# TensorE's first work in a two-branch kernel: four activation groups of the first tokens in four banks, loads in the order tokens, expert rows, tokens, weights

## The chip, the cores and the metric

The kernel runs on one core of one Trainium2 chip. The metric is the device time of one execution in microseconds (us), as the median of several runs. TensorE is written PE, VectorE DVE, ScalarE ACT, GpSimd POOL and SyncE SP, as the profile does.

## The reference

The output mixes two branches over 2048 tokens of width 576, with a gate per token. Branch A is a long convolution per channel whose kernel comes from a state space with 128 states. Branch B routes each token to experts by product keys, and is where most of TensorE's time goes:

```
def _B_ref(x, w_q, k1, k2, u, v):
    q = jnp.einsum("nd,dhc->nhc", xf, w_q)             # 32 heads, two halves of 128
    s1 = jnp.einsum("nhd,ed->nhe", q1, k1)             # 64 keys for each half
    s2 = jnp.einsum("nhd,ed->nhe", q2, k2)
    ... top 2 of s1, top 2 of s2, top 2 of their 4 sums: top_s, top_e
    g = _softmax(top_s, axis=-1)
    act = _gelu(jnp.einsum("nd,nhkd->nhk", xf, u[top_e]))
    out = jnp.einsum("nhk,nhk,nhkd->nd", g, act, v[top_e])

g = sigmoid((x * gate_w).sum(-1))
return g * a + (1 - g) * b
```

There are 64 x 64 = 4096 experts, with rows u and v of width 576.

## The kernel before, in words

**Branch B is computed densely.** The keys are folded into the query weights, so that scores are tokens times a folded matrix (`s` groups: 8 column blocks c times 16 token tiles t, one PSUM bank of 128x512 each). Activations of all experts are tokens times u (`a` groups: 8 expert blocks c times 4 token blocks tb of 512 times 4 quarters j, one bank each). Every operand is split into a high and a low float16 part, so a group is a `triple` (line 850) of 14 matmuls of 512 columns: four 128-row slices of the width 576 times three products (high-high, high-low, low-high), and two more for the last 64 rows. A score group goes to DVE (8 MAX8 and 8 FIND_INDEX8, `scores_top`, line 866). An activation group is scaled by ACT or DVE into a tile `go` and stored to DRAM (`act_post`, line 1247). Later the one-hot products `S` place gates and activations, and the products `o` with v give the output. Branch A runs beside this: a kernel generator on POOL, ACT and DVE (`kP`, `kb`), a first stage (`u`, `k`) and products in frequency (`pr`, `pi`, `pv`).

**One Python planner writes the order.** `body` keeps a clock for TensorE and a `free` time for each other engine; tasks are generators in a heap, and each is resumed when the planner's cost table says that its operands are ready. The main loop (line 1563) puts the next score or activation group on TensorE by rules on DVE's lag and on how many groups of each kind are done. Each engine's program is then a fixed list, run in order, and the waits are semaphores. So a change of the first tasks moves every later instruction a little. All loads and stores stand in SP's one list (line 204).

**The start, before.** SP issues the keys `kt`, the first token block (`xs`, 128x4x512, and its last 64 rows twice in `xr`), two halves of the first query weights `wq`, then the first expert block (`us`, `ur`), then the constants `cst` and the second token block. `x_build(0)` squares the tokens, sums squares on TensorE with a matrix of ones (`x`, five matmuls), derives a power-of-two scale (`root_scale`, line 345: four small DVE operations), and makes the high parts `xb` (TENSOR_SCALAR) and low parts (SCALAR_TENSOR_TENSOR). `w_half` folds the keys into each half of the weights (`w_fold`: 36 small float32 matmuls `wb` on TensorE, each of which is two rows of the trace), finds its scale (`wn`) and makes `whl`. `u_build(0)` does for the experts what `x_build` does for tokens and makes `uhl`, with the last 64 rows in `wrem`. TensorE's first large groups are the scores `s0`, which need `xb` and all of `whl`.

PSUM has eight banks, handed out as tags: four `sc` (for `s` and `a` groups) and four `kb` at this stage. A tag is taken at `bank()` and given back when the reader is done.

Of the kernel before, what the change touches and what calls it, by code (L numbers as in the profile page):

```python
# [116 lines left out]
class Engine:  # L117


    def __init__(self, eng, ready, clock, key, cost):  # L120
        self.eng, self.ready, self.clock, self.key, self.cost = eng, ready, clock, key, cost
        self.free = 0.0

    def __getattr__(self, op):
        f = getattr(self.eng, op)

        def call(*a, **k):
            out = k.get("out", a[0] if a else None)
            aps = [x for x in (*a, *k.values()) if x is not out and hasattr(x, "tensor")]
            start = max(self.free, self.clock[0], *(self.ready.get(self.key(x), 0.0) for x in aps))  # L130
            self.free = start + self.cost(op, out, a, k)
            self.ready[self.key(out)] = max(self.free + 0.28, self.ready.get(self.key(out), 0.0))
# [5 lines left out]
def body(ctx: ExitStack, tc: tile.TileContext, xT, au, par, logdt, dskip, gatew, wq, kT, uT, vv,  # L138
# [283 lines left out]

    def x_load(tb):
# [3 lines left out]
        dma(a, xT[0:512, c].rearrange("(k p) n -> p k n", p=128))  # L427
        dma(r[0:64], xT[512:576, c])
        dma(r[64:128], xT[512:576, c])
        return a, r  # L430
# [15 lines left out]
    def x_build(tb):  # L446
        while tb and tb - 1 not in scaled:
            yield 0.3
        if tb:
            yield from need("slot", 2)  # L450
            xl[tb] = x_load(tb)
        a, r = xl.pop(tb)
        while tb and 0 not in uhl:
            yield 0.3
        b = slot([9, 512], F16, f"xb{tb}")
        sq = b[:, 0:5].bitcast(BF16)
        yield from ready(a, r)
        if tb:
            S.activation(sq[:, 0:4, :], a, AF.Square)
        else:  # L460
            S.activation(sq[:, 0:2, :], a[:, 0:2], AF.Square)
            V.tensor_mul(sq[:, 2:4, :], a[:, 2:4], a[:, 2:4])
        S.activation(sq[:, 4, :], r, AF.Square)
        yield from ready(b)
        yield from need("kb")
        p = bank("kb", f"x{tb}")
        for k in range(5):
            mm(p, onesb, sq[:, k, :], k == 0, k == 4)
        yield from ready(p)
        V.tensor_reduce(out=nx[:, tb:tb + 1], in_=p, axis=AX, op=OP.max)  # L470
        free("kb", nx)
        s, i = root_scale(nx[:, tb:tb + 1], 1.02)
        V.tensor_copy(i_x[:, tb:tb + 1], i)
        yield from ready(s)
        for o, i in [(b[:, k], a[:, k, :]) for k in range(4)] + [(b[:, 8], r)]:
            if tb == 0 or S.free > V.free + 2.0:
                V.tensor_scalar(o, i, s, None, op0=OP.mult)
            else:
                S.activation(o, i, AF.Copy, scale=s)
        scaled.append(tb)  # L480
        for k in range(4):
            yield from ready(b)
# [1201 lines left out]
```

## Time and profile before

| what | value |
|---|---|
| median of 3 runs | 1469.38 us (1467.86 to 1471.87) |
| profiled execution: its own time | 1466.58 us |
| profiled execution: span of instructions | 1464.7 us |
| PE busy | 1431.2 us, 98% of the span |
| DVE busy | 1248.5 us, 85% |
| ACT busy | 790.6 us, 54% |
| POOL busy | 532.0 us, 36% |

The profiled execution lies 1.88 us over its span, and 2.80 us under the median. The page gives busy time by engine and by slices of the span; a view by windows gives the same for stretches that one chooses, with the clock that TensorE was granted (PEclk) and what the DMA engines moved. A row of the timeline holds the start, the duration, the engine, the operation, its tiles and its count, and in brackets the idle time before it and what ended it. Matmul durations overlap, since matmuls are pipelined: the pace is the distance from start to start.

### The profile page before, as it was taken

What the parts mean: (1) busy time and instruction counts of PE and PEld (TensorE: products, weight loads), DVE (VectorE), ACT (ScalarE), POOL (GpSimd) and SP (SyncE); (2) the same over time, 40 slices, a digit from 0 to 9 for tenths busy, and PEclk for the clock granted to TensorE, in tenths of its full rate; (3) what the DMA queues carried; (4) which work ended last, traced back from release to release, by engine and by line L of the source; (5) the groups of instructions that cost most, each with busy time, mean ns of one, the idle gap of its engine ahead of it and who ended that gap; (6) DMA issues with size and microseconds to landing.
All of it is one profiled execution on the core that took longest, in us unless ns stands there. A gap on an engine that the chain in (4) does not pass through costs nothing.

```text
span 1464.7 us, 36789 instructions
## 1 busy us (share of the span) xinstructions
PE 1431.2 (98%) x14025; PEld 858.4 (59%) x14028; DVE 1248.5 (85%) x4589; ACT 790.6 (54%) x1315; POOL 532.0 (36%) x511
## 2 busy tenths in 40 slices
PE   5999999999999999999999999998999999999999
PEld 2445454554544544555555444455787787788787
DVE  6989989989999699959899898579998998898860
ACT  5647767698697787434656544576424224223310
POOL 0443545556745645201246799622100110110100
PEclk8999999999999999999999999999999999999999
DMA  9235433372434534384768666677533432442400
GB/s 319 81 93 162 128 94 118 111 213 89 147 104 133 160 107 135 109 263 138 254 211 290 232 200 206 221 239 221 157 111 116 133 125 85 138 147 68 156 10 17
DMA packets 139185, 221.21 MB, mean 151 GB/s; under 512 B 11648, under 2 KB 82688, under 8 KB 132608
## 3 DMA queue, kind: packets, MB, share of 16 engines
q1 hardware_dynamic: 138912, 218.78, 46.5%
q8 instruction: 110, 1.80, 0.5%
q14 instruction: 67, 0.55, 0.1%
q10 hardware_dynamic: 96, 0.07, 0.0%
HBM read 147.51 MB, written 71.30 MB: 149 GB/s over the span
## 4 chain that ended last, share of the span: by engine, by line
PE 84%; DVE 10%; DMA 3%; ACT 1%; issue 1%; SPq 1%; POOL 1%; DVEq 0%; ACTq 0%; POOLq 0%
PE o L213 24%; PE a L213 23%; PE s L213 22%; PE S L213 4%; PE wb L213 2%; PE kb L213 2%; DVE i L133 2%; PE pr L213 2%; DVE m L133 1%; PE u L213 1%; PE y L213 1%; PE kP L213 1%; DVE e L133 1%; PE pv L213 1%; DVE uh L133 1%
## 5 line engine op out<-in xcount | busy, mean ns | idle before, releaser
L213 PE MATMUL o<-vhl,wh 128*128 128x288 f16 x3072 | 387.0, 286 | 0.0
L213 PE MATMUL s<-whl,xb 128*128 128x512 f16 x1536 | 369.5, 382 | 5.0 <-DVE whl L133 4.2
L213 PE MATMUL a<-xb,uhl 128*128 128x512 f16 x1536 | 361.1, 379 | 0.4 <-DVE ko L133 0.4
L213 PEld LDWEIGHTS <-wh 128*128 128x128 f16 x3072 | 296.0, 98 | 76.3 <-issue 3.7
L213 PEld LDWEIGHTS <-xb 128*128 128x128 f16 x1792 | 171.8, 98 | 213.1 <-issue 27.1
L213 PEld LDWEIGHTS <-uhl 128*128 128x128 f16 x1536 | 148.2, 98 | 175.7 <-issue 2.8
L133 DVE FIND_INDEX8 i<-m,s 128x8 uint32<-128x64 f32 x1024 | 206.5, 222 | 0.0
L133 ACT ACTIVATE wh<-gl,s_wg 128x1024 f16<-128x1024 f32 x64 | 68.9, 1137 | 200.3 <-DVE gl L133 200.3
L133 DVE MAX8 m<-s 128x8 f32<-128x64 f32 x1024 | 146.4, 215 | 28.1 <-PE s L213 27.8
L133 POOL TENSOR_TENSOR CS<-CS,ex 128x512 f32<-128x512 f32 x72 | 100.2, 1423 | 139.0 <-DVE ex L133 120.0
L133 POOL TENSOR_TENSOR ya<-ya,db 128x576 f32<-128x576 f32 x16 | 32.0, 2012 | 305.2 <-DMA ya<-in_au_dram 143.6
L133 ACT ACTIVATE go<-a,i_a 128x512 f32<-128x512 f32 x95 | 64.2, 686 | 82.5 <-PE a L213 54.7
L133 POOL TENSOR_TENSOR e<-aN,rt 128x512 f32<-128x512 f32 x72 | 87.5, 1234 | 50.9 <-PE kb L213 47.6
L133 DVE SCALAR_TENSOR_TENSOR wh<-gl,s_wg,wh 128x1024 f16<-128x1024 f32 x64 | 92.4, 1474 | 11.3 <-ACT wh L133 11.3
L133 DVE TENSOR_TENSOR gl<-S,gl 128x256 f32<-128x256 f32 x256 | 90.0, 415 | 7.3 <-PE S L213 7.3
L133 DVE TENSOR_TENSOR Bg<-Be,vals 128x1024 f16<-128x1024 f16 x128 | 90.6, 749 | 2.2
L133 ACT ACTIVATE gl<-gl 128x1024 f32<-128x1024 f32 x64 | 63.5, 1045 | 34.8 <-DMA gl<-g_d 34.8
L133 DVE TENSOR_TENSOR A<-iota_a,vals 128x2048 f16<-128x2048 f16 x64 | 80.5, 1258 | 0.0
L213 PE MATMUL S<-Bg,A 128*128 128x64 f16 x2048 | 73.0, 193 | 5.1 <-DVE Bg L133 4.2
L213 PEld LDWEIGHTS <-A 128*128 128x128 f16 x2048 | 70.6, 97 | 11.2 <-DVE Bg L133 4.1
L213 PE MATMUL s<-wrem,xb 128*128 128x512 f16 x256 | 76.2, 379 | 0.0
L213 PE MATMUL a<-xb,wrem 128*128 128x512 f16 x256 | 76.2, 379 | 0.0
(203 smaller groups left out, 2205.7 us busy)
## 6 DMA issues: line engine op xcount, KB each, us to landing
g_d<-go SPq DMA_DIRECT2D x128, 256.0 KB, 2.7
gl<-g_d SPq DMA_DIRECT2D x32, 1024.0 KB, 5.4
wq<-in_wq_dram SPq DMA_DIRECT2D x16, 1152.0 KB, 6.3
us<-in_au_dram SPq DMA_DIRECT2D x64, 144.0 KB, 3.0
su_d<-us SPq DMA_DIRECT2D x32, 288.0 KB, 2.6
sk_d<-k1o SPq DMA_DIRECT2D x32, 288.0 KB, 2.8
vn<-in_vv_dram SPq DMA_DIRECT2D x32, 288.0 KB, 3.7
ui<-su_d SPq DMA_DIRECT2D x16, 576.0 KB, 4.0
```

Source lines behind the costliest of these rows:

```text
L133: return f(*a, **k)
L213: T.matmul(o, l, r, start=start, stop=stop)
```

## The change

The loads of the first tokens and of the first expert block are issued ahead of everything else, each as two halves of 128x2x512 behind its remainder; then the keys, the second token block, the weights, the constants. Before the main loop stands a new piece of program that issues the four groups a(0,0,0..3) together, each in its own `sc` bank: for each slice of tokens, four matmuls, one for each bank; first all nine products with the high part of the experts, then the five with the low part. The first scale of tokens and of experts is taken from the sum of all squares that ACT accumulates (`scale_first`), so that it does not wait for the five `x` matmuls. The folds of the weights wait until the second token block is scaled, and lie between these groups. Tokens blocks 1 to 3 get their low parts as each slice is ready, and the second half of a weight block is loaded ahead of the next expert block. The planner's model of an engine that reads what it wrote itself is 0.16 us shorter.

The diff, cut to its core:

```
 class Engine:
+    def at(self, n):
+        t = self.ready.get(n, 0.0)
+        return t - 0.16 if self.own.get(n) == t else t
...
+    def halves_load(a, src, c):
+        columns.add(a.tensor.name)
+        for m in (0, 2):
+            dma(a[:, m:m + 2], src[128 * m:128 * m + 256, c].rearrange("(k p) n -> p k n", p=128))
...
+    def x_first():
+        a, r = xl.pop(0)
+        b = slot([9, 512], F16, "xb0")
+        first_u[1] = b
+        ahead.append(slot([9, 512], F16, "xb1"))
+        sq = ahead[0][:, 0:5].bitcast(BF16)
+        s, i = yield from scale_first(a, r, sq)
+        spawn(x_norm(0, sq))
+        V.tensor_copy(i_x[:, 0:1], i)
+        for k in range(5):
+            while k == 2 and not marks["s"]:
+                yield 0.1
+            o, lo, src = (b[:, k], b[:, 4 + k], a[:, k, :]) if k < 4 else (b[:, 8], b[64:128, 8], r)
+            p = slice(0, 128) if k < 4 else slice(64, 128)
+            V.tensor_scalar(o, src, s, None, op0=OP.mult)
+            V.scalar_tensor_tensor(lo, src[p], s[p], o[p], op0=OP.mult, op1=OP.subtract)
+            marks["x"].append(V.free + 0.28)
...
+    def scale_first(a, r, sq, keep=None):
+        acc = [newcol() for _ in range(3)]
+        yield from ready(r)
+        S.activation(sq[:, 4], r, AF.Square, accum_out=sc[:, acc[0]])
+        for n, m in enumerate((0, 2)):
+            yield from ready(a[:, m:m + 2])
+            S.activation(sq[:, m:m + 2], a[:, m:m + 2], AF.Square, accum_out=sc[:, acc[n + 1]])
+        yield from ready(sq)
+        yield from need("kb")
+        p = bank("kb", "sq")
+        for n in range(3):
+            mm(p[:, 0:1], onesb, short(acc[n].start, 1), n == 0, n == 2, 0.05)
+        yield from ready(p)
+        out = root_scale(p[:, 0:1], 1.02)
...
+    def fold_first(h, w, pbs):
+        while len(folded) < h or 1 not in scaled:
+            yield 0.2
+        out = []
+        yield from need("kb", 3 + h)
+        yield from w_fold(0, h, w, out, ("kb",) * 3)
+        pbs.extend(out)
+        folded.append(h)
...
     def w_half(c, h, w):
...
+        if c == 0:
+            spawn(fold_first(h, w, pbs))
+        while 1 not in scaled:
+            yield 0.2
...
     def u_build(c):
...
+        if c:
+            yield from need("raw")
+            while second:
+                yield 0.3
+                yield from need("raw")
+            take("raw", "raw")
...
+        if c == 0:
+            for k in range(4):
+                S.activation(hl[:, 0, k, :], a[:, k, :], AF.Copy, scale=s)
+                marks["h"].append(S.free + 0.28)
+            S.activation(rem[:, 0, :], r, AF.Copy, scale=s)
...
+            rdy[key(hl)] = marks["h"][k]
+            V.scalar_tensor_tensor(hl[:, 1, k, :], a[:, k, :], s, hl[:, 0, k, :], op0=OP.mult, op1=OP.subtract)
+            marks["u"].append(V.free + 0.28)
...
-    dma(kt, kT)
-    xl = {0: x_load(0)}
+    xl = {0: x_load(0)}
+    take("raw", "raw")
+    xl["u"] = u_load(0)
+    dma(kt, kT)
+    xl[1] = x_load(1)
     w_load(0, 0)
     w_load(0, 1)
+    dma(cst, cst_d[:, :KT])
...
+    until(lambda: marks["x"] and marks["h"], 0.1)
+    first = [bank("sc", f"a0_0_{j}") for j in range(4)]
...
+    for w, n in ((0, 9), (1, 5)):
+        for xk in [x for k in range(4) for x in (k, 4 + k)[:2 - w]] + [8]:
+            k = 4 if xk == 8 else xk % 4
+            landed("x", k)
+            landed("hu"[w], k)
+            for j in range(4):
+                cs = slice(128 * j, 128 * j + 128)
+                mm(first[j], wrems[0][:, w, cs] if k == 4 else first_u[0][:, w, k, cs], first_u[1][:, xk, :],
+                   w == 0 and xk == 0, w == 1 and k == 4)
+            pump()
+    del acts[0:4]
+    for j in range(4):
+        spawn(act_post(0, 0, j, first[j]))
     while groups or acts:
```

SP's list at its start, before (a number in a name ahead of the underscore is the block, behind it a serial number):

```order
L204 DMA kt_113<-in_kT_dram 128x128
L204 DMA xs0_119<-in_xT_dram 128x4x512
L204 DMA xr0_120<-in_xT_dram 64x512 x2
L204 DMA wq0_0_124<-in_wq_dram 128x2304
L204 DMA wq0_1_126<-in_wq_dram 128x2304
L204 DMA us0_142<-in_uT_dram 128x4x512
L204 DMA ur0_143<-in_uT_dram 64x512 x2
L204 DMA cst_70<-in_cst_dram 128x576
L204 DMA xs1_210<-in_xT_dram 128x4x512
```

and of the change:

```order
L211 DMA xr0_119<-in_xT_dram 64x512 x2
L211 DMA xs0_118<-in_xT_dram 128x2x512 x2
L211 DMA ur0_125<-in_uT_dram 64x512 x2
L211 DMA us0_124<-in_uT_dram 128x2x512 x2
L211 DMA kt_113<-in_kT_dram 128x128
L211 DMA xs1_131<-in_xT_dram 128x4x512
L211 DMA xr1_132<-in_xT_dram 64x512 x2
L211 DMA wq0_0_136<-in_wq_dram 128x2304
L211 DMA wq0_1_138<-in_wq_dram 128x2304
```

The experts' block moved ahead of the weights, and the second token block too; both first blocks come in halves.

ACT's list from its first squares on, before (`wj` are squares of the weights, `uhl0` squares and then the high parts of the experts):

```order
L133 ACTIVATE xb0_136<-xs0_119 128x1024
L133 ACTIVATE xb0_136<-xr0_120 128x512
L133 ACTIVATE wj0_0_163,sc_75<-wq0_0_124 128x1152 x2
L133 ACTIVATE wj0_1_223,sc_75<-wq0_1_126 128x1152 x2
L133 ACTIVATE whl0_135<-wb0_0_2_167,sci_76 128x2x256
L133 ACTIVATE wrem2_116<-wb0_0_4_168,sci_76 64x128 x4
L133 ACTIVATE uhl0_282,sc_75<-us0_142 128x2048
L133 ACTIVATE uhl0_282,sc_75<-ur0_143 128x512
```

and of the change:

```order
L140 ACTIVATE xb1_149,sc_75<-xr0_119 128x512
L140 ACTIVATE xb1_149,sc_75<-xs0_118 128x1024 x2
L140 ACTIVATE uhl0_150,sc_75<-ur0_125 128x512
L140 ACTIVATE uhl0_150,sc_75<-us0_124 128x1024 x2
L140 ACTIVATE uhl0_150<-us0_124,sci_76 128x512 x4
L140 ACTIVATE wrem0_114<-ur0_125,sci_76 128x512
L140 ACTIVATE vals_80<-kt_113 128x128
L140 ACTIVATE xb1_149<-xs1_131 128x2048
L140 ACTIVATE xb1_149<-xr1_132 128x512
L140 ACTIVATE xb1_149<-xs1_131,sci_76 128x512 x4
L140 ACTIVATE wj0_0_271,sc_75<-wq0_0_136 128x1152 x2
L140 ACTIVATE wj0_1_313,sc_75<-wq0_1_138 128x1152 x2
```

The squares of the weights moved behind the second token block, and the experts' high parts ahead of both.

PE's list where its large groups begin, before:

```order
L213 MATMUL wn0_1_272<-sc_75,onesb_71 128x1
L213 LDWEIGHTS onesb_71
L213 MATMUL sq_297<-sc_75,onesb_71 128x2
L213 LDWEIGHTS xb0_136
L213 MATMUL s0_0_314<-whl0_135,xb0_136 128x512
```

and of the change:

```order
L220 MATMUL sq_177<-sc_75,onesb_71 128x1
L220 LDWEIGHTS uhl0_150
L220 MATMUL a0_0_0_198<-xb0_148,uhl0_150 128x512
L220 LDWEIGHTS uhl0_150
L220 MATMUL a0_0_1_199<-xb0_148,uhl0_150 128x512
L220 LDWEIGHTS uhl0_150
L220 MATMUL a0_0_2_200<-xb0_148,uhl0_150 128x512
```

The scores `s0` behind both folds are replaced by activation groups ahead of them, one matmul for each bank in turn. Behind the 56 matmuls of these four groups the list of the change has the four groups of the second token block and then the first score group; the 72 fold matmuls `wb` lie in between, 36 behind 40 of the 56, 36 within the second token block. Counted over PE's whole list, both kernels have 1792 matmuls of `s`, 1792 of `a`, 576 of `wb`, 20 of `x`, 2048 of `S` and 3072 of `o`; the change has 13 of `sq` instead of 8. When the last score matmul is issued, 308 matmuls of `a` are left before, and 476 of the change; when the first `S` is issued, 134 and 159.

161 lines of the change are left out of this document (104 added, 57 removed).

## The prediction

> **What bounds the kernel now.** I read the page first (busy time, slices, the chain that ended last), then windows over the start, then its timeline, then the waits of TensorE behind the start.
>
> ```profile
> PE 1431.2 (98%) x14025; PEld 858.4 (59%) x14028; DVE 1248.5 (85%) x4589; ACT 790.6 (54%) x1315; POOL 532.0 (36%) x511
> ...
> PE   5999999999999999999999999998999999999999
> ...
> PE 84%; DVE 10%; DMA 3%; ACT 1%; issue 1%; SPq 1%; POOL 1%; DVEq 0%; ACTq 0%; POOLq 0%
> ```
>
> TensorE is busy for 98% of the span, carries 84% of the chain, and only its first slice is half empty. The windows say how the start differs from the rest:
>
> ```profile
> 0.00:30.67 30.67, 13.54 (x168) 8.19 (x168) 19.71 (x55) 21.02 (x35) 0.20 (x4) 0.83 0.93 331
> 30.67:100.00 69.33, 69.17 (x322) 31.48 (x324) 66.85 (x350) 35.39 (x55) 28.42 (x19) 1.00 0.31 94
> ```
>
> The first figures behind the length are PE's busy time, then PEld, DVE, ACT, POOL, the granted clock, DMA share and GB/s. In the first 30.67 us TensorE works 13.54 us, and DMA is 93% busy; after that it works without a gap. So the place to gain is the start, and what is gained there reaches the end only if TensorE stays the engine that sets the pace. The timeline of the start:
>
> ```profile
> 6.84 1.06 ACT L133 ACTIVATE xb<-xs 128x1024 bf16<-128x1024 f32 x1 [3.75 <-DMA xs<-in_xT_dram]
> 7.95 2.29 PE L213 MATMUL x<-xb,onesb 128*128 128x512 bf16 x5 [4.54 <-ACT xb L133]
> 10.90 3.38 PE L213 MATMUL wb<-kt,wq 128*64 128x64 f32 x72 [0.66 <-DMA wq<-in_wq_dram]
> 11.01 0.15 DVE L133 TENSOR_SCALAR sc<-nx 128x1 f32<-128x1 f32 x1
> 11.71 1.67 DVE L133 TENSOR_SCALAR xb<-xs,sci 128x512 f16<-128x512 f32 x4
> 12.08 1.17 ACT L133 ACTIVATE wj<-wq 128x1152 bf16<-128x1152 f32 x1
> 13.15 0.19 ACT L133 ACTIVATION_READ_ACCUMULATOR wj<-wq 128x1 f32 x1
> 14.35 2.32 PE L213 MATMUL wb<-kt,wq 128*64 128x64 f32 x72
> 15.23 0.74 DVE L133 SCALAR_TENSOR_TENSOR xb<-xs,sci,xb 128x512 f16<-128x512 f32 x1
> 20.84 0.16 PE L213 MATMUL sq<-sc,onesb 128*128 128x2 bf16 x1 [4.04 <-ACT uhl L133]
> 23.47 2.56 ACT L133 ACTIVATE uhl<-us,sci 128x512 f16<-128x512 f32 x4
> 26.34 4.50 PE L213 MATMUL s<-whl,xb 128*128 128x512 f16 x11 [4.20 <-DVE whl L133]
> 30.67 0.59 PE L213 MATMUL s<-wrem,xb 128*128 128x512 f16 x2
> 31.30 1.15 DVE L133 MAX8 m<-s 128x8 f32<-128x64 f32 x8 [2.38 <-PE s L213]
> ```
>
> TensorE's large groups begin at 26.34 (one matmul earlier, at 21.55), because the scores wait for the last low part of the folded weights, `whl`. The eleven matmuls take 4.3 us from start to start, twice their later pace, and these windows show why (0.50 and 1.00 are the granted clock):
>
> ```profile
> 20.10:30.34 10.24, 4.75 (x12) 1.63 (x12) 8.29 (x18) 8.78 (x16) 0.00 (x0) 0.50 0.98 352
> 30.34:40.00 9.66, 9.61 (x45) 4.36 (x45) 7.63 (x62) 3.68 (x6) 0.00 (x0) 1.00 0.53 166
> ```
>
> So the dense stretch at full pace begins at 30.67, with 12 score matmuls, both folds and the norm of the first tokens already done.
>
> **The change, part by part: when the new groups can start.** The loads come first. Bytes by time are read from windows of two microseconds (last figure GB/s), and one landing from the DMA issues:
>
> ```profile
> 0.00:2.00 2.00, 0.00 (x0) 0.10 (x1) 1.00 (x6) 1.26 (x1) 0.20 (x4) 1.00 0.08 22
> 2.00:4.00 2.00, 0.27 (x1) 0.10 (x1) 0.45 (x2) 0.54 (x3) 0.00 (x0) 1.00 0.73 165
> 4.00:6.00 2.00, 0.00 (x0) 0.00 (x0) 0.00 (x0) 0.00 (x0) 0.00 (x0) 1.00 1.04 401
> 6.00:8.00 2.00, 0.05 (x1) 0.04 (x1) 1.16 (x1) 1.16 (x2) 0.00 (x0) 1.00 1.08 345
> 8.00:10.00 2.00, 2.00 (x5) 0.50 (x4) 0.07 (x1) 0.42 (x1) 0.00 (x0) 1.00 1.01 415
> ```
>
> ```profile
> xs<-in_xT_dram SPq DMA_DIRECT2D x1, 1024.0 KB, 5.6
> ```
>
> Two microseconds of each give 0.04, 0.37, 1.18, 1.87 and 2.70 MB by 2, 4, 6, 8 and 10 us. The keys and `xs` are 1.11 MB, moved by 5.8 us; `xs` was issued at 1.19 and landed at 6.8, so a landing is told 1.0 us after its last byte. In the new order tokens are 1.31 MB, landed at 7.4, and tokens with experts 2.62 MB, moved by 9.8 and landed at **10.8 us**. From there on, by the rows above: ACT squares the last half, 1.06, and reads its sum (that row ends 0.10 behind the square): 12.0. Three `sq` matmuls and their way to DVE, about 0.3 as in the row of `sq`: 12.3. `root_scale`, 0.70 from 11.01 to 11.71: 13.0. ACT makes the first high slice, 2.56/4 = 0.64: **TensorE starts at 13.65**. The tokens are no later: from 7.4, ACT 1.2, `sq` 0.3, scale 0.7 give 9.6, and two pairs of high and low slices (1.67/4 + 0.74 each) end at 11.9, before the experts' scale is wanted on DVE. The other pairs (three, 3.5 us) and the experts' low parts (five of 0.74) end near 20, well ahead of the matmuls that read them. Feeding TensorE then costs nothing: the cover is some 24 us of matmuls.
>
> The clock costs something. Before, it rose 4.0 us after the dense start at 26.34, which lost 2.0 us. The first work at 7.95 to 13.3 lost about as much (the first fold took 3.38, the second 2.32). I take 2.3.
>
> By the Trainium skill, TensorE: Matmul & The Clock Gate, section on the HAM clock gate, activity is judged in free-running windows of 3.413 us, and one busy window is needed. The 10.24 us at half clock above are three such windows, so the trace agrees. By that page the half-clock stretch lasts 3.4 to 6.8 us, an estimate of 1.7 to 3.4 us lost instead of 2.3, depending on where the windows fall.
>
> **What is done later than before.** To reach the state of 30.67, TensorE still owes the 12 score matmuls, both folds (2.3 each, 4.6) and the small `wn` and `kn` (0.4). The pace comes from the chain:
>
> ```profile
> 54.60 3.02 PE s L213 x14
> ```
>
> That is 0.216 each, so 12 are 2.6. And there is a new wait: all four groups end with the same last slice, so behind them `a_1_0` needs a bank that ACT has to empty. ACT's list is late there: it squares the second tokens, waits for their scale (TensorE reaches `x` after 24 matmuls, 13.65 + 2.3 + 5.2 = 21.2; then 1.2, 0.7 and 0.7 to 23.8), scales them for 2.6 us and squares the weights for 5.4: 31.8. TensorE ends the four groups at 13.65 + 2.3 + 56 x 0.216 + 1.1 + 2.3 + 0.2 = 31.7. Then `go` takes
>
> ```profile
> L133 ACT ACTIVATE go<-a,i_a 128x512 f32<-128x512 f32 x95 | 64.2, 686 | 82.5 <-PE a L213 54.7
> ```
>
> 0.69 us. Behind the stopped matmul stands all of TensorE's list. I take 1.5 us for this and for the second fold's banks, with bounds of 0 and 3 (four of these evictions in a row). Four banks in turn, 128x512 matmuls each, is a form that no row shows; a row of 14 in one bank has 0.216, so I take no gain and no cost.
>
> **Sum.** 13.65 + 2.3 + 2.6 + 4.6 + 0.4 + 1.5 = 25.05, against 30.67: **5.6 us less** at the start. The profiled execution took 1466.58, its span and 1.88 around it; 1466.58 - 5.6 = 1461.0. It lies 2.8 under the median of the runs, so for a median I say 1463.7.
>
> **What follows.** The planner writes the whole list anew, so every later wait is drawn again. These are TensorE's waits from 31 us on:
>
> ```profile
> PE S L213 <- DVE Bg L133: 4.2, 6, 2.3
> PE pi L213 <- DVE m L133: 1.7, 1, 1.7
> PE k L213 <- ACT k1o L133: 1.4, 1, 1.4
> PE y L213 <- DMA tf<-in_tf_dram: 1.0, 1, 1.0
> PE kb L213 <- issue: 1.0, 1, 1.0
> PE u L213 <- DVE uh L133: 0.7, 2, 0.5
> PE S L213 <- DVE ya L133: 0.7, 1, 0.7
> PE k L213 <- DVE i L133: 0.6, 1, 0.6
> ```
>
> With three smaller ones they are 12.4 us. They can fall away or come twice, so their change lies between -12.4 and +12.4; I take zero, since the numbers of matmuls are the same.
>
> **Rivals.** First, **more than the start**. Near 1000 us DVE is the bound:
>
> ```profile
> 1002.00:1060.00 58.00, 52.34 (x612) 40.04 (x610) 57.69 (x86) 27.24 (x32) 12.90 (x8) 1.00 0.60 188
> ```
>
> It works 57.69 of 58 us, and TensorE waits there 4.2 + 0.7 for `Bg` and `ya`. The change keeps 476 `a` matmuls for the time behind the scores instead of 308, which is 36 us more cover. If that removes these waits, the median is 1458.8. Against it: at the first `S` only 25 more are left, 5.4 us.
>
> Second, **the gain is eaten by new waits**: half as much again as the 12.4 us leaves 1463.7 + 6.2 = 1469.9, no change. For it: the list is in order and one late operand stops all; against it: 12.4 us in 1430 shows that the planner's costs are near the chip's.
>
> Third, **DVE becomes the bound, and it is slower**. The first MAX8 moves from 31.30 to about 52: 112 `a` and 14 `s` matmuls, ten `x`, folds and losses behind 13.65. DVE was idle for 31.3 - 19.7 = 11.6 us before its first score. Of the change it works some 32 by then (an estimate: the 67 rows of its list ahead of the first MAX8, at the durations above), and is idle for 20. If scores set the pace up to the products, the difference of some 9 us comes on top of the old time: 1469.4 + 9 = 1478. It decides once no activation group is left to fill. Against it: the spare 476 matmuls at the end of the scores.
>
> Fourth, **the early start fails**. If the experts land with the weights as late as before, TensorE starts some 3 us later: 1466.6. Or the four banks keep the clock low: 56 matmuls at half pace cost 12.1 more, less the 2.3 counted, 1473.5. The Trainium skill, TensorE: Matmul & The Clock Gate, section on psum-queue depth-cycling, reports such a clock for bursts that change banks; no run here shows it for these groups.
>
> **How the numbers follow.** The forecast, a gain of 3.5 to 8 us at the start that is kept (1461.4 to 1465.9), has 0.52. More: 0.16. Eaten: 0.20. DVE the bound: 0.08. Early start fails: 0.04. A measurement of this kernel can tell about 0.3%, 4.4 us. Faster by more than that are 0.16 and most of the forecast, 0.44, together 0.60; slower are 0.08 and 0.02; 0.30 lie between. The range takes 8 us to each side, past more cover and the eaten gain, and leaves out the worst of the bounds: 1455.5 to 1471.5.
>
> **What would show it.** First `a` matmul at 13 to 14.5 us; the granted clock full by 17.5 to 19; a wait of about 1 us for `go` near 32; first MAX8 near 52; PE at 99% of 60 to 1000 us. Wrong: more than 3 us of idle time in 13 to 50, TensorE waiting for MAX8 or FIND_INDEX8 before 1000, or waits behind 60 us that add up to 18 or more.

## The result, and the profile after

The changed kernel takes **1488.50 us** (median of 6 runs, 1484.56 to 1491.61); the kernel before, on the same chip, 1468.81 (6 runs, 1466.06 to 1471.87). The ratio is **1.013, with a 95% interval of 1.0109 to 1.015**: slower by 1.3%, where a gain of 5.6 us was forecast. The profiled execution took 1485.77 us with a span of 1484.0, which is 19.3 us more than the span before.

The page shows little of it at first sight: TensorE's share fell by one point, the first slice of PE is fuller, and only the chain of what ended last says that more of the time runs over DVE (17% against 10%) and POOL.

```profile
PE 1437.2 (97%) x14033; PEld 861.0 (58%) x14033; DVE 1255.9 (85%) x4609; ACT 777.5 (52%) x1295; POOL 533.5 (36%) x511
...
PE   6999999999999999999999999999999999999999
...
PE 73%; DVE 17%; POOL 4%; DMA 2%; issue 2%; ACT 1%; SPq 0%; DVEq 0%; POOLq 0%; ACTq 0%
```

**The start did what it was to do.** TensorE's timeline, with DVE's first MAX8 as its last row:

```profile
14.38 4.11 PE L220 MATMUL a<-xb,uhl 128*128 128x512 f16 x12 [1.44 <-ACT uhl L140]
18.39 2.75 PE L220 MATMUL a<-xb,uhl 128*128 128x512 f16 x12
...
25.60 2.32 PE L220 MATMUL wb<-kt,wq 128*64 128x64 f32 x72
27.85 2.76 PE L220 MATMUL a<-xb,uhl 128*128 128x512 f16 x12
...
32.52 0.81 PE L220 MATMUL a<-xb,uhl 128*128 128x512 f16 x3 [0.96 <-ACT go L140]
...
53.20 1.14 DVE L140 MAX8 m<-s 128x8 f32<-128x64 f32 x8
```

How far it gained is counted best by matmuls: windows of the first 60 us for the tiles `a` and `s` alone, PE's busy time with the number of matmuls in brackets. Before:

```profile
0.00:60.00 60.00, 14.98 (x68) 0.91 0.62 213
...
0.00:60.00 60.00, 17.93 (x70) 0.91 0.62 213
```

And after:

```profile
0.00:60.00 60.00, 29.39 (x124) 1.00 0.69 230
...
0.00:60.00 60.00, 9.23 (x42) 1.00 0.69 230
```

That is 166 matmuls of these groups against 138. Both kernels have done both folds, and the changed one has also done two `x` more, 17 against 15 (the trace before shows 13, but two of its three fives stand there as four in the time of five): 30 times 0.216 us are **6.5 us ahead at 60 us**. (The expectations of the experiments speak of 8 to 9 us. They were worked out with a typical duration for each kind of matmul, and that of the single `kn` held a wait; the count is right, and all their amounts lost from the start on shift by the same 2 us.)

**The loss comes behind it, in pieces.** TensorE's idle time from 60 us on is read from the windows, length minus the first figure. Before:

```profile
60.00:130.00 70.00, 69.48 (x395) 33.13 (x395) 65.47 (x353) 33.36 (x57) 32.27 (x25) 1.00 0.39 117
130.00:300.00 170.00, 170.00 (x1656) 86.41 (x1655) 153.80 (x552) 125.17 (x185) 85.32 (x69) 1.00 0.41 125
300.00:740.00 440.00, 435.68 (x4044) 224.33 (x4042) 381.49 (x1734) 304.34 (x513) 189.83 (x191) 1.00 0.49 155
740.00:960.00 220.00, 218.33 (x2054) 106.19 (x2053) 186.44 (x1119) 117.25 (x309) 164.12 (x188) 0.99 0.67 228
960.00:1090.00 130.00, 124.34 (x1381) 87.76 (x1380) 121.99 (x187) 68.69 (x89) 24.69 (x16) 1.00 0.57 181
```

After:

```profile
60.00:130.00 70.00, 64.41 (x298) 29.44 (x297) 68.73 (x384) 29.79 (x53) 29.70 (x23) 0.95 0.36 107
130.00:300.00 170.00, 166.13 (x1582) 84.61 (x1581) 159.47 (x579) 132.15 (x194) 81.86 (x66) 1.00 0.43 130
300.00:740.00 440.00, 433.57 (x4203) 223.88 (x4202) 394.31 (x1943) 288.19 (x485) 193.89 (x193) 1.00 0.43 138
740.00:960.00 220.00, 212.01 (x2000) 104.12 (x2000) 174.30 (x922) 118.18 (x319) 165.47 (x193) 1.00 0.72 239
960.00:1090.00 130.00, 123.22 (x1195) 80.09 (x1194) 113.14 (x170) 63.26 (x79) 25.38 (x14) 0.96 0.58 182
```

| us of the span | idle before | idle after | clock after, and what it cost |
|---|---|---|---|
| 60 to 130 | 0.5 | 5.6 | 0.95; two stretches of 3.4 us at half clock: 3.4 |
| 130 to 300 | 0.0 | 3.9 | 1.00 |
| 300 to 740 | 4.3 | 6.4 | 1.00 |
| 740 to 960 | 1.7 (and one stretch of 3.4 us at half clock: 1.7) | 8.0 | 1.00 |
| 960 to 1090 | 5.7 | 6.8 | 0.96; one stretch of 3.4 us and one of 6.8: 5.1 |

Behind 1090 us both work without a gap but for the last 4 us. The table's rows add up to 18.5 us of new idle time to 1090 us and 6.8 us of clock (half the length of each stretch at half clock), 25.3 of the 6.5 + 19.3 = 25.8 us that were lost. The clock is a follower: four waits of 2.1 to 3.5 us each have a stretch at half clock behind them, which costs 1.7 us, and 3.4 us after the last. In windows cut at the places where the granted clock changes:

```profile
85.40:88.80 3.40, 3.40 (x10) 1.20 (x9) 3.40 (x30) 0.00 (x0) 1.14 (x1) 0.50 0.00 0
...
1044.60:1051.40 6.80, 5.91 (x49) 4.32 (x50) 6.77 (x14) 0.00 (x0) 0.00 (x0) 0.50 0.01 2
```

The first follows the wait of 3.5 us at 80.8, the second one of 3.3 us for `Bg`. The waits of TensorE behind 60 us (total, times, longest), of 14 kinds that add up to 30.8 us:

```profile
PE S L220 <- DVE Bg L140: 6.8, 6, 3.3
PE u L220 <- DVE uh L140: 5.0, 4, 2.1
PE sq L220 <- ACT uhl L140: 3.8, 2, 3.5
PE s L220 <- DVE i L140: 2.6, 2, 2.1
```

How a wait that names ACT is DVE's: ACT's rows around 80 us, and then TensorE's.

```profile
79.90 0.26 ACT L140 ACTIVATE vals<-m 128x64 f32<-128x64 f32 x1 [2.74 <-DVE m L140]
81.49 0.26 ACT L140 ACTIVATE idx<-i 128x64 f16<-128x64 uint32 x1 [1.33 <-DVE i L140]
81.65 1.89 ACT L140 ACTIVATE uhl<-us 128x2048 bf16<-128x2048 f32 x1
83.45 0.19 ACT L140 ACTIVATION_READ_ACCUMULATOR uhl<-us 128x1 f32 x1
83.54 0.61 ACT L140 ACTIVATE uhl<-ur 128x512 bf16<-128x512 f32 x1
```

```profile
84.30 0.16 PE L220 MATMUL sq<-sc,onesb 128*128 128x2 bf16 x1 [3.51 <-ACT uhl L140]
```

ACT's list holds the copies of the first four score groups' results, for which it stands 2.74 us (MAX8) and 1.33 us (FIND_INDEX8), and the squares of the second expert block stand behind those copies. TensorE's `sq` waits for the squares, and behind `sq` stands everything else.

### The profile page after: what moved, and what is told of

Read it like the earlier page. It is cut to its first block, busy times and chain, and to the rows that moved or that the text cites. A ratio compares the mean times of both kernels' runs of the same rounds, so it can differ in the third digit from the quotient of the medians.

```text
span 1484.0 us, 36824 instructions
## 1 busy us (share of the span) xinstructions
PE 1437.2 (97%) x14033; PEld 861.0 (58%) x14033; DVE 1255.9 (85%) x4609; ACT 777.5 (52%) x1295; POOL 533.5 (36%) x511
## 4 chain that ended last, share of the span: by engine, by line
PE 73%; DVE 17%; POOL 4%; DMA 2%; issue 2%; ACT 1%; SPq 0%; DVEq 0%; POOLq 0%; ACTq 0%
PE o L220 23%; PE a L220 18%; PE s L220 18%; PE S L220 4%; DVE i L140 3%; PE wb L220 2%; POOL vf L140 2%; DVE m L140 2%; PE kb L220 2%; DVE e L140 1%; DVE uh L140 1%; DVE Y L140 1%; PE y L220 1%; DMA g_d<-go 1%; DVE CS L140 1%
## 5 line engine op out<-in xcount | busy, mean ns | idle before, releaser
L140 POOL TENSOR_TENSOR CS<-CS,ex 128x512 f32<-128x512 f32 x72 | 96.5, 1372 | 143.9 <-DVE ex L140 114.5
L140 ACT ACTIVATE go<-a,i_a 128x512 f32<-128x512 f32 x86 | 58.1, 683 | 85.3 <-PE a L220 57.5
L140 DVE TENSOR_TENSOR Bg<-Be,vals 128x1024 f16<-128x1024 f16 x128 | 86.1, 714 | 2.2
L220 PEld LDWEIGHTS <-A 128*128 128x128 f16 x2048 | 72.1, 98 | 12.6 <-DVE Bg L140 6.2
```

The lines of the kernel that those rows point to most:

```text
L140: return f(*a, **k)
L220: T.matmul(o, l, r, start=start, stop=stop)
```

## Experiments

The theories. **D**: scores start 20 us later on DVE, which then runs in debt, and TensorE waits for what stands in DVE's and ACT's lists behind score work. **L**: each newly planned list draws its own waits, and the list before is a tight one. **G**: the new gate (`while len(scaled) < 4`) holds up the second expert block. **P**: the planner's 0.16 us is too optimistic. **S**, formed later: the products S lack activation matmuls to lie between. The table holds all runs; each was compared with the kernel before on its own chip (1467.12 to 1467.92 us there). Idle time is TensorE's in the profiled execution, from windows of 60 to 960 and 960 to 1090 us, the clock that of the second.

| kernel | us | ratio, 95% interval | idle 60-960 | idle 960-1090, clock |
|---|---|---|---|---|
| before (its profile above) | 1468.81 | | 6.5 | 5.7, 1.00 |
| changed | 1488.50 | 1.013 (1.0109-1.015) | 23.9 | 6.8, 0.96 |
| a_no_gate | 1503.61 | 1.0237 (1.0216-1.0258) | 32.2 | 10.7, 0.96 |
| a_no_second | 1483.95 | 1.0108 (1.0089-1.0126) | 20.9 | 3.7, 0.99 |
| a_wire | 1485.29 | 1.013 (1.010-1.016) | 22.3 | 3.0, 1.00 |
| b_wire | 1466.86 | 0.9991 (0.9981-1.0001) | 6.6 | 4.5, 1.00 |
| a_no_index | 1479.16 | 1.0086 (1.0058-1.0115) | 18.4 | 8.7, 0.97 |
| d_b_no_index | 1466.03 | 0.9992 (0.998-1.0003) | 5.7 | 4.1, 0.99 |
| a_no_at | 1489.05 | 1.0147 (1.012-1.0174) | 9.1 | 22.3, 0.92 |
| b_at | 1498.53 | 1.0221 (1.0187-1.0256) | 29.4 | 3.8, 0.99 |
| a_weights_first | 1480.55 | 1.0085 (1.0057-1.0112) | 20.6 | 5.2, 0.97 |
| c_keep48 | 1492.85 | 1.0175 (1.0158-1.0192) | 21.4 | 16.1, 0.93 |
| c_start_only | 1477.85 | 1.007 (1.0054-1.0087) | 13.0 | 8.7, 0.97 |
| c_start_keep40 | 1485.26 | 1.0122 (1.0105-1.0138) | 25.6 | 1.7, 1.00 |
| c_b_keep40 | 1480.70 | 1.0097 (1.008-1.0114) | 20.2 | 2.2, 1.00 |
| d_b_half | 1462.08 | 0.9962 (0.9951-0.9973) | 6.9 | 4.1, 0.99 |
| d_a_half | 1471.91 | 1.0029 (1.0008-1.0049) | 10.8 | 8.0, 0.97 |
| d_start_half | 1468.78 | 1.0021 (1.0009-1.0033) | 6.2 | 7.3, 1.00 |
| e_b_no_gw | 1461.22 | 0.9949 (0.9932-0.9967) | 3.6 | 4.1, 0.99 |
| e_a_no_gw | 1463.55 | 0.9975 (0.9963-0.9987) | 5.7 | 8.5, 0.97 |

### The gates: a_no_gate and a_no_second

The changed kernel without one of its new gates each. The first:

```
-        while len(scaled) < 4:
-            yield 0.3
```

The second, in `u_build`:

```
-            while second:
-                yield 0.3
-                yield from need("raw")
```

> The changed kernel without the wait that lets the second expert block be built only when all four token blocks are scaled; its load then stands before the third token block. Theory G (the late second expert block leaves only scores behind 67 us): the waits of 3.5 and 2.1 us at 80 and 116 us and the half clock behind them go, some 8 us, so about 1480. Theory D (the first 16 score groups start 20 us later, and DVE must do them in less time before expert block 1 begins, whatever is loaded): the loss in 70 to 120 us stays at 5 to 8 us, 1485 to 1489. Theory L (each newly planned list draws its own waits): anywhere within 10 us of 1488, with waits at other places.

> The changed kernel without the rule that an expert block waits for the second half of a weight block. Up to 300 us its list is the same, so the first 8 us are lost as before. If the rule is to blame for the 8 us lost in 740 to 850 us (296 score matmuls left at the products, where 495 were left before the change), then with 523 left it is about 1480. Theory L: within 10 us of 1488, with no tie to the count of scores.

Theory G fell: without the gate the kernel is 15 us slower still, which no theory had foreseen (D's 1485 to 1489 and L's 10 us are missed as well). Its waits name DVE, as in the changed kernel, and are larger:

```profile
PE u L220 <- DVE uh L140: 22.7, 4, 13.5
```

`u` is a small step of branch A. It waits for `uh`, a SCALAR_TENSOR_TENSOR that stands behind scores in DVE's list. Without the second gate the time falls by 4.6 us, half of the way to the 1480 that was named, and the start's loss stays. TensorE still idles 6.5 us from 740 to 960 us, against 8.0 with the gate: that gate, and the number of scores that it leaves for this stretch, is no main cause.

### A small move of the lists: a_wire and b_wire

```
-        wire[0] = max(wire[0], t) + 4 * o.shape[0] * size(o) / 3.4e5
+        wire[0] = max(wire[0], t) + 4 * o.shape[0] * size(o) / 3.3e5
```

> The changed kernel with nothing but one number of the planner's model moved: the rate of transfers 3.3e5 instead of 3.4e5. The program does the same work in another order. Theory L: differs from 1488 by 3 to 10 us either way. Theories D and G: the loss at 70 to 120 us stays 5 to 8 us, and the total stays within 3 us of 1488.

> The kernel before with the same number of the planner's model moved. Theory L: differs from 1469 by 3 to 15 us, likely slower, since the list before was one of few with so few waits. Theories D and G: within 3 us of 1469.

The planner then takes loads for a little longer, and some instructions move. Both kernels all but kept their times (a_wire lies 3.2 us under the changed kernel, where D and G allowed 3 and L spoke of 3 to 10), so L in its simplest form, that any new list is some 10 us off, is not so.

### DVE's debt at the start: a_no_index and its control d_b_no_index

```
-            V.max_index(out=i8[:, q, g, :], ...)
+            (V.no_max_index if c == 0 else V.max_index)(out=i8[:, q, g, :], ...)
```

The planner counts these 128 FIND_INDEX8 as before, so that every list keeps its order, but they are not issued.

> The changed kernel with the same lists on every engine, except that DVE's 128 FIND_INDEX8 of the first 16 score groups are not issued (the planner still counts them; four small memsets are added), so that the indices of these groups are left out of what is computed. DVE has some 26 us less to do in 51 to 122 us. Theory D (DVE has that stretch full, since scores start 20 us later, and TensorE waits for it): the waits at 80 and 116 us go, TensorE stays 8 us ahead of the kernel before until 120 us of work, and the time falls by 6 to 9, to about 1480. Theory G or a late ACT or DMA: the waits stay, within 2 us of 1488.

> The kernel before without the 128 FIND_INDEX8 of the first 16 score groups, the order unchanged, and with 4 memsets; the indices of these groups are left out. The same edit made the changed kernel 5.8 us faster (1479.16 against 1484.95 in that batch's terms, 9.3 less than the changed kernel's median). Theory D (the first 8 us of loss belong to the late first scores of the change): within 3 us of the kernel before, which loses 1.5 us at that place. If it gains 5 or more as well, DVE's debt is no peculiarity of the change.

(Of the two amounts in the second text, 9.3 is the one that counts, from the median of 1488.50.) In the changed kernel the window from 60 to 130 us is now without a gap:

```profile
60.00:130.00 70.00, 70.00 (x395) 33.88 (x395) 52.17 (x187) 34.62 (x62) 32.44 (x25) 1.00 0.42 126
```

DVE works 52.2 us where it worked 68.7, and TensorE 70.0 at full clock where it worked 64.4 at 0.95. That is 5.6 + 3.4 = 9.0 us, and the time fell by 9.3 (8.5, when each is taken against the kernel before on its own chip). The same edit in the kernel before is worth 1.2 us, within the scatter. So **DVE's load is shown for the first part of the loss, about 9 us**: these waits come from it, and only in the changed kernel. That it is the late scores that put DVE in debt is not shown by this; the next two sections bear on it. What was lost behind 130 us stayed.

### The planner's 0.16 us: a_no_at and b_at

In the changed kernel it is taken out, and in the kernel before it is put in, alone:

```
     def at(self, n):
         t = self.ready.get(n, 0.0)
-        return t - 0.16 if self.own.get(n) == t else t
+        return t
```

> The changed kernel with the planner's old model of an engine that reads what it wrote itself (without the 0.16 us). Theory P (the shorter model makes the planner expect operands too early, so that waits come all along the list): the losses behind 120 us of work shrink from 76 to 58 us as in the kernel before, to about 1472; the first 8 us stay lost. Theory D alone: within 4 us of 1488.

> The kernel before with nothing but that model of the change (0.16 us). Theory P: slower by 5 to 15 us, 1474 to 1483. Otherwise: 1467 within 3 us.

The number alone costs the kernel before 30 us: its idle time from 60 to 960 us goes from 6.5 to 29.4, with no other part of the change. So P holds for that list, at twice the size that it named. In the changed kernel the median does not move, and yet the loss does. These are the windows of 60 to 960 and 960 to 1090 us of a_no_at:

```profile
60.00:960.00 900.00, 890.91 (x8073) 447.42 (x8073) 795.89 (x3796) 561.17 (x1031) 468.66 (x471) 1.00 0.49 157
960.00:1090.00 130.00, 107.73 (x1179) 73.00 (x1178) 118.16 (x184) 72.61 (x103) 31.47 (x19) 0.92 0.58 195
```

To 960 us it idles 9.1 us, little more than before. Then it idles 22.3 us at a clock of 0.92, while DVE is busy 118 of 130 us, above all with `Bg`, `gl` and `A`. The waits of this stretch are 13.7 us for `Bg` and 8.0 for `vhl`, most of it DVE's: what TensorE had won it gave back where it waits for DVE. (DVE's share alone doesn't tell this; the kernel before has 122 of 130 us there and idles 5.7.) At the first S only 95 activation matmuls were left, against 134 before and 159 in the changed kernel; that made theory S.

### Weights ahead of the second tokens: a_weights_first

```
+    w_load(0, 0)
+    w_load(0, 1)
     xl[1] = x_load(1)
-    w_load(0, 0)
-    w_load(0, 1)
```

The folds, the weights' squares and the first `x` reduction no longer wait for the second tokens' scale either.

> The changed kernel with the weights loaded ahead of the second token block, and the folds and the norm of the first tokens not held until the second block is scaled, so that scores can begin earlier. Theory D: if the first MAX8 comes at 40 instead of 51, DVE has up to 10 us more before 122, and that much of the early gain is kept, about 1480; the early fold stands ahead of the first groups on TensorE and waits for the weights' landing, which costs 3 to 5 at the start. Theory P or L: no better than 1485.

It is 8 us faster than the changed kernel and still 12.6 slower than the one before on the same chip. D's 1480 was met, but not in D's way: the first MAX8 comes at 45.47 us, not at 40, and from 60 to 130 us TensorE still idles 5.7 us. One wait of 3.9 us stays at 73 us, and it again is `sq`, this time put down to DVE's `i`. c_start_only of the next section differs from this kernel in the planner's 0.16 us alone. These are the windows of a_weights_first and of c_start_only:

```profile
60.00:130.00 70.00, 64.26 (x364) 30.54 (x363) 68.77 (x393) 31.98 (x57) 24.47 (x18) 0.98 0.39 119
60.00:130.00 70.00, 69.27 (x392) 33.03 (x392) 65.44 (x348) 29.02 (x52) 21.21 (x16) 1.00 0.40 120
```

So the late scores are not the whole reason for DVE's debt at the start. Put side by side, with one profiled execution each:

| kernel | planner's number | first MAX8 | idle 60-130, clock |
|---|---|---|---|
| before | old | 31.30 | 0.5, 1.00 |
| b_at | 0.16 less | 32.83 | 4.1, 0.98 |
| c_start_only | old | 44.83 | 0.7, 1.00 |
| a_weights_first | 0.16 less | 45.47 | 5.7, 0.98 |
| a_no_at | old | 52.25 | 3.4, 1.00 |
| changed | 0.16 less | 53.20 | 5.6, 0.95 |

With the old number the first scores come 13.5 us later for 0.7 us of idle time there, and 21 us later for 3.4; with the new number the stretch loses 4 us or more wherever they begin.

### More filler for S: c_keep48, c_start_only, c_start_keep40, c_b_keep40

The rule in the main loop, with 48 in a_no_at's program, and 40 in two others:

```
-        a_ok = a_ok and (len(acts) > 26 or not groups or groups[0][0] not in whl)
+        a_ok = a_ok and (len(acts) > 48 or not groups or groups[0][0] not in whl)
```

c_start_only is a_weights_first without the 0.16 us, which leaves of the change the early loads and the four groups.

> The changed kernel without the planner's 0.16 us, and the planner keeps 48 activation groups for the time behind the scores instead of 26; the same work in another order. The kernel with only the first of these was ahead of the kernel before up to 940 us of TensorE's work (60.1 us lost to waits and clock against 62.3) and lost 31 in the next 40, where only 95 activation matmuls were left to lie between the products S. Theory S (that loss is want of filler): some 165 are left now, the stretch costs what it costs the kernel before, about 15, and the median is 1463 to 1472. Theory L (each newly planned list draws its waits, whatever its filler): anywhere from 1475 to 1500, with waits at new places.

> The changed kernel with two of its parts undone: the planner's 0.16 us is taken out, and the first weights are loaded ahead of the second tokens and folded at once, so that TensorE's first scores come earlier. What is left of the change is the early loads of tokens and experts and the four groups in four banks. Theory D (the later scores let DVE run into debt, and only the start is to blame for the first loss) expects less lost between 70 and 120 us of TensorE's work than the 9.8 us of the changed kernel, 5 or under. For the whole: if the planner's 0.16 us is the worst part, 1466 to 1474; if every new list loses to the one before (theory L), 1475 to 1490.

> The kernel of the run ahead of this one with 40 activation groups kept for the time behind the scores instead of 26. Both have about as much filler at the first S (activation matmuls left: 156 and 162), so theory S expects the same stretch of S in both, within 4 us. Theory L: the lists differ from the middle on, and so do the medians, by 5 us or more either way.

> The kernel before with 40 activation groups kept instead of 26, and nothing of the change. At the first S it has 156 activation matmuls left, the kernel before 134. Theory S: the same time or a little less, 1462 to 1469. Theory L (the list before is an unusually tight one, and a planner's number alone draws a worse one, as 0.16 us did for 30 us): 1475 to 1495, with no part of the change in it.

**Theory S fell**, and the medians of all four runs lie in the ranges that L had named. c_start_keep40's stretch of S differs from that of c_start_only by 7 us of idle time, where S allowed 4. (D's small first loss is met by c_start_only, which idles nowhere from 70 to 120 us.) c_keep48 had its filler at the first S and still idled 16.1 us from 960 to 1090; its waits:

```profile
PE S L220 <- DVE Bg L140: 14.2, 8, 9.2
PE u L220 <- DVE uh L140: 13.9, 5, 10.9
```

The second row is the price of the filler: groups held back for later are missing near 540 us, scores follow one another, DVE falls behind and `u` waits 10.9 us for `uh`. The kernel before pays the same for 40 kept groups, with nothing of the change in it (10.8 us for `uh`, 10.1 of it once, and 13 us in the median). c_start_only is the best of all versions with the start of the change, 10.6 us over the kernel before; the same start with 40 kept loses 7.4 more. So a planner's rule that seems to have no cost is worth 5 to 30 us here, and no version beats the kernel before.

### DVE's load as such: d_b_half, d_a_half, d_start_half

```
-            V.max_index(out=i8[:, q, g, :], ...)
+            (V.no_max_index if g % 2 else V.max_index)(out=i8[:, q, g, :], ...)
```

> The kernel before with every other FIND_INDEX8 of the scores not issued (512 of 1024, with their MATCH_VALUE_LOAD: 140 us of DVE's 1248) and 32 memsets of the index tiles; the order on every engine is the same, since the planner still counts them. Half of the indices are left out. It is the control of the next run: if TensorE is the bound in the kernel before, as its 98% say, it stays within 5 us of 1467; if DVE sets part of the time there too, it falls by 10 or more.

> The changed kernel with the same 512 FIND_INDEX8 not issued and the same memsets; the order of every engine is that of the changed kernel. Half of the indices are left out. Theory D (TensorE's lead is lost because DVE, in debt behind the late scores, can't follow): with DVE relieved the gain of the start comes through, and this kernel is 4 to 9 us faster than the one ahead of it. Theory L (the new list draws waits on ACT, POOL and DMA, and DVE's load has little to do with it): it stays 10 us or more slower than the one ahead of it.

> The start-only kernel (early loads and the four groups in four banks, weights ahead of the second tokens, the planner's model as before) with the same 512 FIND_INDEX8 not issued. Undisturbed it took 1477.85. Theory D: 2 to 6 us faster than the kernel before with the same instructions left out, since its start is 4 us ahead. Theory L: 5 us or more slower than that kernel.

The kernel before falls by 5.1 us, next to the 5 that were named for TensorE as the bound and far from the 10 for DVE: TensorE is its bound in the main, as its page said. (The profiled execution of d_b_half took 1467.09 us, 5.0 over its median, so its windows don't show where the 5.1 us were gained.) The changed kernel falls by 16.6, the start-only one by 9.1. What is left between changed and before is 9.8 us, half of the 19.7; for start-only 6.7 of 10.6. D's numbers were missed: it foresaw a gain for both. L's 10 us or more for the changed kernel were missed by little, and its 5 or more for the start-only kernel were met. The windows of d_a_half show where D holds and where not:

```profile
60.00:130.00 70.00, 69.34 (x341) 32.50 (x340) 68.03 (x310) 33.34 (x61) 32.57 (x25) 1.00 0.40 120
740.00:960.00 220.00, 214.63 (x1944) 103.79 (x1943) 152.93 (x631) 118.24 (x309) 166.05 (x182) 1.00 0.71 239
960.00:1090.00 130.00, 122.00 (x1293) 84.37 (x1292) 116.64 (x174) 62.20 (x73) 25.20 (x13) 0.97 0.59 189
```

To 130 us the gap is all but gone, and so are the waits for `uh`. From 740 to 960 TensorE idles 5.4 us although DVE is busy for only 153 of 220 us; the kernel before with the same edit idles 0.0 there. From 960 to 1090, where no FIND_INDEX8 is left to take out, it idles 8.0 at a clock of 0.97, with DVE busy 117 of 130 us. So DVE's load explains half, and the products needed an experiment of their own.

### POOL's load in the products: e_a_no_gw and e_b_no_gw

What ACT waits for from 740 to 960 us tells the two lists apart (engine and tile, what it waits for, total, times, longest). Before:

```profile
ACT tt L133 <- PE pi L213: 37.8, 19, 3.9
ACT tt L133 <- POOL vf L133: 17.2, 6, 3.9
```

And in the changed kernel:

```profile
ACT tt L140 <- POOL vf L140: 27.4, 11, 3.8
ACT tt L140 <- PE pi L220: 13.9, 8, 2.8
```

Before, ACT waited above all for TensorE, which then had the lead; now for POOL, whose busy time is the same (164 and 165 of 220 us). To take some of POOL's load away, its 16 products `vn<-vn,gw` are not issued, in d_a_half and in d_b_half alike, with all lists unchanged:

```
-                G.tensor_mul(a, a, gw)
+                G.no_tensor_mul(a, a, gw)
```

> The changed kernel with half of the FIND_INDEX8 left out, and also POOL's 16 products vn<-vn,gw not issued (23 us of POOL's time from 740 to 960 us); the order of every engine stays. Left out are half of the indices and the gate's weights. If POOL holds up the products (its vf and vn are what ACT waits for, and TensorE waits for ACT's tt), TensorE's idle time from 740 to 960 us falls from 5.4 to 2.5 or less and the median from 1471.9 to 1469 or less. If the list's layout alone does it, whatever POOL's load, it stays within 1.5 us of 1471.9.

> The control: the kernel before with the same instructions left out. Its products have no idle time with half of the FIND_INDEX8 left out, so by either theory it stays within 1.5 us of 1462.1.

The changed kernel falls by 8.4 us, the kernel before by 0.9. The window from 740 to 960 us of the first:

```profile
740.00:960.00 220.00, 219.38 (x2037) 106.94 (x2035) 150.34 (x637) 124.32 (x314) 142.24 (x166) 1.00 0.74 252
```

Idle time there goes from 5.4 to 0.6 us and the median to 1463.55, as the theory of POOL had it (2.5 and 1469 or less). Since the list is the same, a matmul can be followed from one trace to the other: an `s` that starts at 848.67 us in d_a_half starts at 847.68 here, and an `a` at 908.81 starts at 899.74. So 8.1 of the 9.1 us between the two profiled executions are gained in these 60 us of the products, and behind them the distance stays as it is. What stays stands in S:

```profile
PE S L221 <- DVE Bg L141: 8.4, 8, 4.3
```

**What is settled, and what not.** The changed kernel lay 19.7 us over the one before. With half of the FIND_INDEX8 gone from both it is 9.8, and with POOL's 23 us gone too, 2.3 (1463.55 against 1461.22). But for what was left out, the lists of every engine were the same all the while. So 9.9 us of the difference hang on DVE's load and 7.5 on POOL's: shown, for this order of taking away (POOL's part was not taken away alone), and to the 1 to 2 us by which such medians scatter. DVE's debt from 60 to 130 us is the part of its 9.9 that has a place, about 9; the late scores and the planner's number make it together. That the waits for `Bg` in S eat what is left of the lead is read from the windows, and was not taken away by a run. For the stretch to 130 us the planner's 0.16 us has a share in this. Open is what in the new list puts POOL's work, and the rest of DVE's, where TensorE has to wait for it, since both do the same work in both kernels. It is neither gate, and want of activation matmuls isn't it.

## Why the prediction was wrong

1. **Loads**: told for 10.8 us, ACT takes up the experts' last half at 11.58; 0.8 late. The first `a` came at 14.38 against 13.65, inside the bounds that were named (13 to 14.5).
2. **Clock**: 2.3 us were set for it. The first 12 `a` matmuls take 4.01 us from start to start (14.38 to 18.39), 12 at 0.216 take 2.59: 1.4. The clock rose at 17.06, 2.7 us behind the first `a`, where the prediction's estimate was a stretch of 3.4 to 6.8.
3. **Four banks in turn**: no gain and no cost was taken. Twelve of them go from 27.85 to 30.45, which is 0.217 each; the fourth rival falls. The Trainium skill, TensorE: Matmul & The Clock Gate, section on psum-queue depth-cycling, tells of a kernel that cycles through banks, in which TensorE is idle for moments between its groups and the clock goes back and forth. These groups change the bank at each matmul without idle time between them, and the trace shows no such clock.
4. **The new bank wait**: 1.5 for `go` near 32; measured 0.96 at 32.52.
5. **The sum of the start**: 5.6 less; measured 6.5 ahead at 60 us. Right, with a clock and a bank wait that cost less than was set for them and loads that were later. (Two small slips: 1461.0 + 2.8 is 1463.8, and the third rival's 20 - 11.6 is 8.4, not 9.)
6. **"What follows"** is the step that failed. It said "their change lies between -12.4 and +12.4; I take zero, since the numbers of matmuls are the same". Idle time to 1090 us grew by 18.5 us and half clock behind it took 6.8 more. The second rival had new waits eat the gain, at 6.2 us and with a chance of 0.20; that is what happened, at three times the idle time. The number of matmuls says nothing about whether their operands are there in time. A list that is planned anew isn't drawn evenly around the old one either: of eleven other orders that were tried, one (b_wire) was as good as the list before, and the others were 10 to 36 us slower, two of them (b_at and c_b_keep40, by 31 and 13) without any part of the new start. And "12.4 us in 1430 shows that the planner's costs are near the chip's" was read wrongly: the small sum belonged to that one list. A planner's number that moved by 0.16 us cost it 30.
7. **The third rival was right that DVE becomes the bound, and far too cheap.** Its count held to the letter: first MAX8 at 53.20 against "about 52", and DVE idle for 20.5 us before it against 20, by this window:

```profile
0.00:53.20 53.20, 40.77 (x306) 20.37 (x307) 32.70 (x82) 33.87 (x57) 12.73 (x13) 1.00 0.74 247
```

DVE then is busy 68.7 of 70 us and still cannot keep up. It had a chance of 0.08 because of "the spare 476 matmuls at the end of the scores", and "It decides once no activation group is left to fill". Both are wrong. At 80 us nearly all activation groups were still to come, and none could be put in: the list is fixed, the next one stood behind a wait, and the second expert block itself (`uhl`) hung on ACT's copies of DVE's results. Filler helps only if it stands at that place in the list and its own operands do not pass through the engine that is late. Its price, 9 us for the later start, was about what the first stretch cost, and that is in part luck: 3.4 of these 9.0 us are the clock, which the rival did not count, and the stretch takes the planner's new number as well as the late scores, which alone cost 0.7 to 3.4 us of idle time there. The rest is from step 6, and most of it hangs on POOL, which no rival named.
8. **The first rival** hoped for fewer waits at the products S, since activations were kept. They grew, from 4.2 to 6.8 us for `Bg`, and in a_no_at and c_keep48, which had 95 and 165 activation matmuls left there, to 13.7 and 14.2.

What was to show it wrong did so: the waits behind 60 us add up to 30.8, over the 18 that were named, and TensorE waited 7.2 us for MAX8 and FIND_INDEX8 before 1000. (The second sign tells little: the kernel before waits 2.3 us for them.)

## What to carry to other kernels

In this kernel the earlier start of the engine that is busy for 98% was lost because the engines that feed it could not follow, DVE (85%) and POOL (36% of the span, but 75% of the products); so ask of such a start what it does to their idle time before their first work, and where the first engine's list waits for them. In a program with fixed lists, filler counts by its place and by what its operands pass through, not by how much of it is left. And before a planner's list is changed, move one of its numbers alone in the old kernel: what that costs (here 0, 13 and 31 us for three numbers) is the scale of the term "everything behind it", and it belongs into the range.

## What the runs showed of the hardware

- In the changed kernel, waits of TensorE of 3.5, 2.1 and 2.1 us (at 80.8, 116.1 and 1014.9) were each followed by 3.4 us at half clock, and one of 3.3 us at 1041.9 by 6.8 us. Each of these stretches costs half its length. The Trainium skill, TensorE: Matmul & The Clock Gate, section on the HAM clock gate, has activity judged in windows of 3.413 us; the lengths here are one and two of these, so the trace agrees. The length of a wait alone doesn't decide whether this follows: behind a wait of 2.1 us near 831 (`s` for DVE's `i`) the clock stayed at 1.00 to 840, while in the kernel before one of 1.7 us at 887 was followed by 3.4 us at half clock.
- The granted clock in the profile's windows can be blind at the very start. It reads 1.00 from 13.64 to 17.06 us, while the first matmuls there start 0.40 to 0.43 us apart, twice the later 0.216; go by the pace there.

```profile
13.64:17.06 3.42, 2.67 (x7) 1.02 (x8) 3.31 (x6) 3.42 (x7) 0.00 (x0) 1.00 1.07 377
```
